# Eleven units of a second MLP product by seven block products instead of eight, on one Trainium2 core

## The chip, the cores and the metric

The kernel runs on one core of one Trainium2 chip. Five engines work beside each other: TensorE (PE, whose weight loads the profile lists as PEld), VectorE (DVE), ScalarE (ACT), GpSimd (POOL) and SyncE (SP, which issues the DMAs here). Each engine takes its instructions in an order that is fixed when the program is built, and waits on semaphores for the others. The metric is the device time of one execution in microseconds. The kernel before takes 416.2 us (median of three runs, 416.14 to 416.21).

## The reference

The input `x` has 2048 tokens of 448 columns. Its layer norm `xn` goes two ways, and everything is added up:

```python
x  = A_x
xn = _layernorm(x)
return x + A(xn) + B(xn)

def A(x):                       # a filter in the frequency domain
    X = rfft2(x); X = X * (w_r + 1j * w_i)
    return irfft2(X, s=(S, D))

def B(x):
    h  = gelu(layernorm(x) @ w1)
    # four column quarters shifted by +1, -1, +2, -2 tokens
    x1 = x + concat(shifted quarters of h) @ w2
    h2 = gelu(layernorm(x1) @ w3) @ w4      # w3: 448 x 1792, w4: 1792 x 448
    return x1 + h2
```

The change concerns only the last product, `gelu(...) @ w4`, for the last two groups of tokens.

## The kernel before

**Number format.** Every large product is made of three fp16 passes: each operand is split into a high and a low half, and high x high, high x low and low x high are added up in fp32 in PSUM (`PASS`). A split is one ACT copy to fp16 (the high half) and one DVE operation that subtracts it (the low half). `powers` forms powers of two that bring an operand into fp16's range; `s4` and `r4` are those of w4.

**The MLP.** The 2048 tokens are 16 blocks of 128, and a group `G` of 0 to 7 is two blocks. F = 1792 is cut into 14 chunks of 128, and a unit `(G, fp)` is one group with two chunks, so there are 8 x 7 = 56 units. A unit has two halves:

- `front(G, fp)` (L691) makes the hidden values: 22 matmuls of 256 columns (in `mlp_in`, L381) into a PSUM bank `pw` of tag "mm", of which there are two. Behind them ACT applies the gelu in place (L698) and copies the high half to `hf` (L700), and DVE makes the low half (L701).
- `back(G, fp)` (L705) multiplies by w4: for each of two blocks, two chunks and three passes, one matmul of 448 columns, 12 in all (L720), into two banks `acc` that add up over a group's seven units. In group 7 the last block is done in two column halves in two banks, so there are 6 matmuls of 448 columns and 12 of 224. Behind the group's last unit DVE adds the banks to the running sum `xt` (L726), and for groups 6 and 7 SP sends the block out (L729).

`mlp` (L731) issues the units of some groups in order, with `ahead` fronts in front of each back.

**The order of the work.** The program is written in stages, but each engine's order comes from a planner that simulates the program when it is built: of the instructions that are ready in its simulation, it takes the one of the lowest priority number. The stages' own instructions have the numbers of their place in the text; the MLP's matmuls have a high number (`FILL`), so that they fill what the stages leave free on PE; the copies behind a front have the lowest (`EVAC`). `behind(...)` makes an instruction wait in that order for another one.

**The stages around the change.** After the frequency filter's chunks comes the inverse transform: for each of the 16 blocks `inv_a` (L658, matmuls L663 into `pe`, banks of tag "tr", and sums in one of two buffers `stage0` and `stage1`, even blocks in the one and odd blocks in the other) and `inv_b` (L680, matmuls L684 into `py`, banks of tag "sp"), whose result is added to `xt`; `finish` (L494) sends blocks 0 to 11 out. The buffer `y1` (32 KB of each partition) is read for the last time in the inverse. In the text, `mlp(range(3, 6))` stands ahead of the inverse and `mlp(range(6, 8))` behind it, and then nothing follows. w4's split halves lie in `w4p`, and its raw values were loaded early in the kernel to `x2mem`, which later holds the transposed inputs of all fronts.

Of the kernel before, what the change touches and what calls it, by code (L numbers as in the profile page):

```python
# [12 lines left out]
F32 = mybir.dt.float32  # L13
F16 = mybir.dt.float16
I32 = mybir.dt.int32
AF = mybir.ActivationFunctionType
ALU = mybir.AluOpType
AX = mybir.AxisListType

S, D, DF, F = 2048, 448, 225, 1792  # L20
# [4 lines left out]
PASS = ((0, 0), (0, 1), (1, 0))  # L25
# [10 lines left out]
WMAX = [(1, 4), (1, 5), (1, 6), (2, 0), (2, 1), (2, 2), (2, 3), (2, 4)]  # L36
HS = 3
EVAC, FILL = 0, 100000

ME = [0, 224] + list(range(2, 224, 2))  # L40
MO = list(range(1, 224, 2))
# [78 lines left out]
def body(tc, nc, x, wf, w1, w2, w3, w4, c_g, c_n, c_small, out):  # L120
    V, A, P, T, SY = nc.vector, nc.scalar, nc.gpsimd, nc.tensor, nc.sync
    PSUM = bass.MemoryType.PSUM

    @contextlib.contextmanager
    def prio(base):
        kept = tc.cur_priority
        tc.cur_priority = max(base, at.get(base, 0))
        yield
        at[base] = tc.cur_priority
        tc.cur_priority = kept  # L130

    at = {}
    opened = {}

    def pool(name, bufs=1, side="left", space=None):
        kw = dict(name=name, bufs=bufs, reuse_waits="tile")
        if space is not None:
            kw["space"] = space
        else:
            kw["side"] = side  # L140
        cm = tc.tile_pool(**kw)
        opened[name] = cm
        return cm.__enter__()

    def close(name):
        opened.pop(name).__exit__(None, None, None)

    ps = pool("ps", space=PSUM)

    def bank(tag, name):  # L150
        return ps.tile([128, 512], F32, tag=tag, bufs=2, name=name)

    pc = pool("pc")
    px = pool("px")
    pw = pool("pw")
    pa = pool("pa")
# [3 lines left out]
    xt = [px.tile([128, 2, D], F32, name=f"xt{i}") for i in range(8)]  # L160

    def xb(b):
        return xt[b // 2][:, b % 2]
# [4 lines left out]
    def stage(name, n, side, dtype=F32):  # L168
        t = pw.tile([128, 1808], F32, tag=f"stage{side}", bufs=1, name=name)
        return (t if dtype is F32 else t.bitcast(dtype))[:, :n]  # L170
# [46 lines left out]
    x2mem = pw.tile([128, 9 * F], F16, name="x2mem")  # L217
    x2all = x2mem[:, 0:8 * F].rearrange("p (j t n) -> p j t n", j=4, t=7)
    w4raw = x2mem.bitcast(F32)[:, F:].rearrange("p (f n) -> p f n", f=14)
    w4v = w4.rearrange("(f p) n -> p f n", p=128)  # L220
# [16 lines left out]
        junk = xr.bitcast(F16) if junk is None else junk  # L237
        A.activation(out=junk[:src.shape[0], :n], in_=src, func=AF.Square, scale=2.0 ** -20, accum_out=col)

    def powers(m, n, key, tag="acc"):  # L240

        t = pc.tile([128, 2], F32, name=f"pt{key}")
        V.tensor_reduce(out=t[:, 0:1], in_=m[:, :n], axis=AX.X, op=ALU.add)
        pm = bank(tag, f"pm{key}") if isinstance(tag, str) else tag
        i = T.matmul(pm[:, 0:1], ones, t[:, 0:1], start=True, stop=True)
        after["p" + key] = (i.ins,)
        V.tensor_scalar(out=t[:, 1:2], in0=pm[:, 0:1], scalar1=2.0 ** -58, scalar2=None, op0=ALU.max)
        e = pc.tile([128, 3], I32, name=f"pe{key}")
        V.tensor_scalar(out=e[:, 0:1], in0=t.bitcast(I32)[:, 1:2], scalar1=1, scalar2=0x7F800000,
                        op0=ALU.logical_shift_right, op1=ALU.bitwise_and)  # L250
        V.tensor_scalar(out=e[:, 1:2], in0=e[:, 0:1], scalar1=-1, scalar2=185 << 23, op0=ALU.mult, op1=ALU.add)
        V.tensor_scalar(out=e[:, 2:3], in0=e[:, 0:1], scalar1=1, scalar2=69 << 23, op0=ALU.mult, op1=ALU.add)
        return e.bitcast(F32)[:, 1:2], e.bitcast(F32)[:, 2:3]

    def absmax(out_, in_):
# [2 lines left out]
    def split_w(hi, lo, src, s, low=None):  # L258
        if low is P:
            P.tensor_scalar(out=src, in0=src, scalar1=s, scalar2=0.0, op0=ALU.mult, op1=ALU.add)  # L260
            i = A.activation(out=hi, in_=src, func=AF.Copy)
            j = P.tensor_tensor(out=lo, in0=src, in1=hi, op=ALU.subtract)
            return i.ins, j.ins
        i = A.activation(out=hi, in_=src, func=AF.Copy, scale=s)
        j = V.scalar_tensor_tensor(out=lo, in0=src, scalar=s, in1=hi, op0=ALU.mult, op1=ALU.subtract)
        return i.ins, j.ins
# [86 lines left out]
    after = {}  # L353

    @contextlib.contextmanager
    def behind(*key):
        key = key if len(key) > 1 else key[0]
        with contextlib.ExitStack() as st:
            for i in after[key]:
                st.enter_context(tc.issue_after(i))  # L360
            yield
# [21 lines left out]


    w3p = pa.tile([128, 8, F], F16, name="w3p")
    w4p = {}

    w1p = p1.tile([128, 8, D], F16, name="w1p")
    w2p = pr.tile([112, 2, 4, D], F16, name="w2p")
# [299 lines left out]
    acc, hs = {}, {}  # L689

    def front(G, fp, tag):  # L691
        tok = slice(256 * (G % 2), 256 * (G % 2) + 256)
        pm = bank(tag, f"pw3_{G}{fp}")
        for ff in range(2):
            f = 2 * fp + ff
            mlp_in(pm[:, 256 * ff:256 * ff + 256], w3p, slice(128 * f, 128 * f + 128), x2all[:, G // 2], tok)
        with prio(EVAC):
            A.activation(out=pm, in_=pm, func=AF.Gelu_apprx_tanh, scale=r3)  # L698
            h = pw.tile([128, 2, 512], F16, tag="hf", bufs=3, name=f"hf{G}{fp}")
            i = A.activation(out=h[:, 0], in_=pm, func=AF.Copy, scale=h3)  # L700
            j = V.scalar_tensor_tensor(out=h[:, 1], in0=pm, scalar=h3, in1=h[:, 0], op0=ALU.mult, op1=ALU.subtract)  # L701
            after["f", G, fp] = i.ins, j.ins
        hs[G, fp] = h

    def back(G, fp):  # L705
        h = hs.pop((G, fp))
        if fp == 0:
            acc[G] = [bank("acc", f"acc{G}{i}") for i in range(2)]
            if G == 7:
                acc[G].append(bank("sp", "acc72"))  # L710
        for i in range(2):
            b = 2 * G + i
            c = D // 2 if b == NB - 1 else D
            parts = [(slice(o, o + c), acc[G][i + o // c][:, 0:c]) for o in range(0, D, c)]
            for r, to in parts:
                with behind("m", G, fp) if (G, fp) == (7, 6) and ("m", G, fp) in after else contextlib.nullcontext():
                    for f in (2 * fp, 2 * fp + 1):
                        for n, (hi, wi) in enumerate(((0, 0), (0, 1), (1, 0))):
                            o = 256 * (f % 2) + 128 * i
                            m = T.matmul(to, h[:, hi, o:o + 128], w4p[0][:, wi, f, r],  # L720
                                         start=f == 0 and n == 0, stop=f == 13 and n == 2)
                after["m", G, fp] = (m.ins,)
            if fp == 6:
                with prio(EVAC):
                    for r, to in parts:
                        V.scalar_tensor_tensor(out=xb(b)[:, r], in0=to, scalar=p34[:, min(G, 1):min(G, 1) + 1],  # L726
                                               in1=xb(b)[:, r], op0=ALU.mult, op1=ALU.add)
                        if G > 5:
                            SY.dma_start(ov[:, b, r], xb(b)[:, r])  # L729

    def mlp(Gs, hook=None, ahead=1, tags=("mm",)):  # L731
        with prio(FILL):
            todo = [(G, fp) for G in Gs for fp in range(7)]
            done = 0
            for n, (G, fp) in enumerate(todo):
                while done < min(n + 1 + ahead, len(todo)):
                    front(*todo[done], tags[done % len(tags)])
                    if hook:
                        with prio(EVAC):
                            hook(*todo[done])  # L740
                    done += 1
                back(G, fp)
# [9 lines left out]
    m1, m2, m3, m4 = (pc.tile([128, n], F32, name=f"m{i}") for i, n in ((1, 4), (2, 1), (3, 4), (4, 7)))  # L752
# [35 lines left out]
    with behind("n", 0):  # L788
        s1, r1 = powers(m1, 4, "1", "mm")
    h_alloc(0)  # L790
    first = [bank("mm" if k < 2 else "sp", f"pw1_0{k}") for k in range(4)]
# [51 lines left out]
    s3, r3 = powers(m3, 4, "3", "mm")  # L843
    h3 = pc.tile([128, 1], F32, name="h3")
# [22 lines left out]
        w1_unit(3, k)  # L867
    with behind("h", 3, 3):
        SY.dma_start(csm, c_small)
    s4, r4 = powers(m4, 7, "4")  # L870
    p34 = pc.tile([128, 2], F32, name="p34")
    V.scalar_tensor_tensor(out=p34[:, 1:2], in0=r3, scalar=2.0 ** 5, in1=r4, op0=ALU.mult, op1=ALU.mult)
    V.tensor_tensor(out=p34[:, 0:1], in0=p34[:, 1:2], in1=s12[:, 0:1], op=ALU.mult)
    w4p[0] = pa.tile([128, 2, 14, D], F16, tag="R", bufs=1, name="w4p")
    with behind(3, 1):
        w4_split(0)
    with behind(3, 3):
# [18 lines left out]
    pa2 = pool("pa2")  # L896
# [42 lines left out]
        if 0 <= i - 3 < NC:  # L939
            chunk_c(i - 3)  # L940
    close("pst")
    mlp(range(3, 6))
    pv = pool("pv", side="right")
    bs = [*range(8), *range(12, 16), *range(8, 12)]
    for n in range(17):
        if n in (0, 8):
            gather_u(n)
        if n < 16:
            inv_a(bs[n])
        if n:  # L950
            b = bs[n - 1]
            inv_b(b)
            if b < 12:
                finish(b)
    mlp(range(6, 8))
    for name in ("pv", "pa2", "pa", "pw", "px", "pc", "ps"):
        close(name)


# [22 lines left out]
```

## Time and profile before

| | |
|---|---|
| median of three runs | 416.2 us |
| the profiled execution | 416.43 us |
| its span, from the first instruction to the last | 414.6 us |
| granted TensorE clock, mean | 0.999 |
| instructions | 8472 |
| `front` matmuls (L381) | 1232, 151.7 us busy |
| `back` matmuls (L720) | 714, 139.7 us busy |
| inverse, from the first `pe` matmul to the last `py` | 284 to 338 us |
| MLP alone on PE | 339 to 411 us |
| from the last `back` matmuls' start (36 of them) | 406.8 us |

How to read it: the page gives the busy time of each engine, 40 equal slices of the span, the chain of work that ended last (followed back from the last instruction), and groups of instructions with count, busy time, mean duration and the idle time ahead of them. Matmul durations are modelled and overlap, so the distance between the starts of steps says more than the busy time. In the chain and the timeline a row is a run of like instructions: start, length, engine, what it writes, line, count.

### The profile page before, as it was taken

How to read it: one execution, taken by the hardware profiler on the slowest of the kernel's cores; microseconds unless marked ns; L12 is line 12 of the kernel's file. 1: busy time of each engine (PE TensorE's matmuls, PEld its weight loads, DVE VectorE, ACT ScalarE, POOL GpSimd, SP SyncE). 2: the span in 40 equal slices, each digit the busy share in tenths (PEclk: the TensorE clock that was granted, in tenths of full speed). 3: DMA queues.
4: the chain of work that ended last, by engine and by line, in shares of the span. 5: the costliest groups of instructions: out<-in, count | busy, mean ns of one | idle time of the engine just before them, and what ended most of it. 6: DMA issues, size and time to landing. Idle time of an engine off the chain costs nothing.

```text
span 414.6 us, 8472 instructions
## 1 busy us (share of the span) xinstructions
PE 407.9 (98%) x3313; PEld 290.4 (70%) x3313; DVE 294.3 (71%) x613; ACT 246.1 (59%) x428; POOL 97.2 (23%) x172
## 2 busy tenths in 40 slices
PE   8999999999989999999999999999999999999996
PEld 3655555765658777776888887877777766777885
DVE  4888899798866879854799888857999934112122
ACT  4698879973758876643689888854344533222321
POOL 3876710102245947400021122110000000000000
PEclk9999999999999999999999999999999999999999
DMA  8959879914867557315256655500111011001001
GB/s 275 350 189 177 159 148 323 158 59 90 186 166 206 153 183 221 90 47 141 70 149 163 168 144 141 127 27 2 69 46 66 2 47 44 2 0 46 2 0 46
DMA packets 54536, 48.53 MB, mean 117 GB/s; under 512 B 37536, under 2 KB 48864, under 8 KB 54496
## 3 DMA queue, kind: packets, MB, share of 16 engines
q1 hardware_dynamic: 54496, 47.99, 43.6%
q8 instruction: 26, 0.43, 0.4%
q14 instruction: 14, 0.11, 0.1%
HBM read 35.52 MB, written 3.67 MB: 95 GB/s over the span
## 4 chain that ended last, share of the span: by engine, by line
PE 68%; DVE 12%; ACT 7%; issue 4%; DMA 4%; POOL 2%; SPq 1%; DVEq 0%; POOLq 0%; ACTq 0%
PE pw L381 26%; PE acc L720 25%; PE pw L410 4%; PE ps L539 3%; PE pe L663 2%; PE wps L749 2%; PE py L684 2%; ACT te L619 2%; DVE xt L452 2%; DMA x2mem<-y 2%; DMA x2mem<-w 1%; PE pu L642 1%; PE pp L597 1%; DVE y L484 1%; PE px L614 1%
## 5 line engine op out<-in xcount | busy, mean ns | idle before, releaser
L381 PE MATMUL pw<-x2mem,w3p 128*128 128x256 f16 x1232 | 151.7, 273 | 0.0
L720 PE MATMUL acc<-w4p,hf 128*128 128x448 f16 (+1 forms) x714 | 139.7, 341 | 1.4 <-DVE hf L701 1.4
L381 PEld LDWEIGHTS <-w3p 128*128 128x128 f16 x1232 | 119.0, 98 | 22.4
L720 PEld LDWEIGHTS <-hf 128*128 128x128 f16 x714 | 69.2, 98 | 49.9 <-DVE hf L701 1.8
L701 DVE SCALAR_TENSOR_TENSOR hf<-pw,h,hf 128x512 f16<-128x512 f32 x56 | 41.8, 747 | 64.1 <-ACT hf L700 63.7
L698 ACT ACTIVATE pw<-pw,pe 128x512 f32<-128x512 f32 x56 | 36.7, 656 | 76.8 <-PE pw L381 76.6
L450 PE MATMUL pw<-w2p,h 112*128 112x448 f16 x192 | 39.9, 352 | 0.7 <-DMA h<-hs 0.7
L700 ACT ACTIVATE hf<-pw,h 128x512 f16<-128x512 f32 x56 | 38.3, 687 | 1.5
L410 PE MATMUL pw<-w1p,xT 128*128 128x448 f16 x176 | 35.4, 352 | 0.0
L623 POOL TENSOR_TENSOR z<-te 128x450 f32<-128x450 f32 x16 | 15.7, 982 | 69.5 <-DVE te L621 69.5
L450 PEld LDWEIGHTS <-h 112*128 112x128 f16 x192 | 18.6, 98 | 17.2 <-DMA h<-hs 1.0
L410 PEld LDWEIGHTS <-xT 128*128 128x128 f16 x176 | 16.9, 98 | 16.4 <-DVE xT L375 0.8
L604 ACT ACTIVATE pf<-pp 64x450 f16<-64x450 f32 x32 | 17.4, 543 | 12.6 <-DVE pf L605 8.3
L605 DVE TENSOR_TENSOR pf<-pp,pf 64x450 f16<-64x450 f32 x32 | 19.9, 622 | 4.3 <-ACT pf L604 3.9
L522 POOL TENSOR_TENSOR f<-xr 128x452 f32<-128x452 f32 x16 | 18.4, 1173 | 0.6
L619 ACT ACTIVATE te<-px 64x450 f32<-64x450 f32 x32 | 17.3, 540 | 1.1 <-PE px L614 0.6
L726 DVE SCALAR_TENSOR_TENSOR xt<-acc,p,xt 128x448 f32<-128x448 f32 (+1 forms) x17 | 10.9, 651 | 8.6 <-PE acc L720 8.3
L530 DVE TENSOR_TENSOR xh<-f,xh 128x452 f16<-128x452 f32 x16 | 12.6, 828 | 5.5 <-ACT xh L529 5.5
L519 POOL TENSOR_TENSOR xr<-xf 128x452 f32<-128x452 f32 x8 | 9.9, 1236 | 26.0 <-issue 20.2
L529 ACT ACTIVATE xh<-f 128x452 f16<-128x452 f32 x16 | 8.4, 571 | 10.3 <-POOL f L522 10.2
L684 PE MATMUL py<-vh,csm 128*128 128x448 f16 x48 | 14.0, 352 | 0.0
L663 PE MATMUL pe<-csm,U 113*128 113x113 f16 (+1 forms) x192 | 13.7, 213 | 0.0
(164 smaller groups left out, 572.5 us busy)
## 6 DMA issues: line engine op xcount, KB each, us to landing
wc<-wf SPq DMA_DIRECT2D x32, 225.0 KB, 3.7
wl<-wf SPq DMA_DIRECT2D x8, 450.0 KB, 4.0
xt<-x SPq DMA_DIRECT2D x8, 448.0 KB, 9.0
xf<-x SPq DMA_DIRECT2D x8, 448.0 KB, 3.9
loads<-x SPq DMA_DIRECT2D x7, 448.0 KB, 3.7
out<-xt SPq DMA_DIRECT2D x13, 224.0 KB, 1.9
w3raw<-w SPq DMA_DIRECT2D x3, 896.0 KB, 13.7
gn<-c_g SPq DMA_DIRECT2D x16, 128.0 KB, 3.1
```

The costliest lines, as they stand in the source:

```text
L381: T.matmul(ps_out, wp[:, wi + t, cols], xT[:, xi + t, tok], start=t == 0 and wi + xi == 0, stop=t == 3 and wi == 4)
L410: T.matmul(pm[:, :D], xTs[g][:, xi + t, 128 * i:128 * i + 128], w1p[:, wi + t], start=t == 0 and p == 0, stop=t == 3 and p == 2)
L450: T.matmul(pm[:, :D], hT[g][:112, 4 * hi + k, o:o + 128], w2p[:, wi, k], start=n == 0, stop=n == 11)
L522: P.tensor_tensor(out=f[:, :, k:k + 2].rearrange("p b s d -> p s b d"), in0=u[:, :, 0], in1=u[:, :, 1], op=op)
L605: V.tensor_tensor(out=lo, in0=src, in1=hi, op=ALU.subtract)
L619: A.activation(out=e[64 * h:64 * h + 64], in_=px_[64 - 64 * h:128 - 64 * h, :2 * DF], func=AF.Copy)
L663: T.matmul(pe[:, 113 * q:113 * q + 113], U[b // 8 * 8][ui][:kd, q, b % 8, :], cI[ii][:kd, 113 * q:113 * q + 113], start=n == 0, stop=n == 2)
L684: T.matmul(py[:, :D], cV[ri], vh[:, vi], start=n == 0, stop=n == 2)
L698: A.activation(out=pm, in_=pm, func=AF.Gelu_apprx_tanh, scale=r3)
L700: i = A.activation(out=h[:, 0], in_=pm, func=AF.Copy, scale=h3)
L701: j = V.scalar_tensor_tensor(out=h[:, 1], in0=pm, scalar=h3, in1=h[:, 0], op0=ALU.mult, op1=ALU.subtract)
L720: m = T.matmul(to, h[:, hi, o:o + 128], w4p[0][:, wi, f, r], start=f == 0 and n == 0, stop=f == 13 and n == 2)
```

## The change

Six units of group 6 (all but the last) and five of group 7 (0, 1, 2, 4, 5) multiply by w4 in another way. A unit is a product of a 2 x 2 block matrix (two token blocks by two chunks, blocks of 128 x 128) with another (two chunks by two column halves, blocks of 128 x 224). The plain way takes eight block products; the new one takes seven, of sums and differences of blocks, and adds their results up.

- `sums` takes the place of the copies behind such a unit's front: the gelu goes from PSUM to an fp32 buffer `g` in SBUF, two DVE operations form the sums, and the high and low halves (`hz`) are made of all seven operands, 896 columns instead of 512.
- `w4_sums` loads a pair of w4's chunks again (448 KB) into `stage0` or `stage1`, forms their differences and sums with four DVE operations of 224 columns, and splits the 896 columns. This is done for six pairs of chunks, behind the units (5,4), (5,5), (5,6), (6,0), (6,1) and (6,3). The results lie in parts of `x2mem` and of w4's buffer that are free by then. w4's scale is one power of two smaller, to leave room for the sums.
- `seven` takes the place of `back` for these units: 7 x 3 = 21 matmuls of 224 columns. Four of the products add up over the units in two more banks (`side`, of tag "tr" in group 6 and "sp" in group 7), and behind a group's last such unit five DVE operations add them to `xt`. Group 7's third bank moves from "sp" to "tr".
- Group 5 is issued behind the inverse, and its two blocks go out behind its last unit instead of in `finish`. `y1` is given up ahead of it, and its place is taken by the new buffers `g` and `hz`.
- Groups 6 and 7 are issued with two fronts ahead of each back instead of one, and with one for unit (7,5). Group 7's order is 0, 1, 2, 4, 5, 3, 6, so that its last two units are plain ones.

```diff
+SEVEN = {6: [0, 1, 2, 3, 4, 5], 7: [0, 1, 2, 4, 5]}
+ORD = {G: list(range(7)) for G in range(6)} | {6: list(range(7)), 7: [0, 1, 2, 4, 5, 3, 6]}
...
+    def sums(G, fp, pm):
+        g = pz.tile([128, 12, 128], F32, tag="g", bufs=2, name=f"g{G}{fp}")
+        q = g.rearrange("p (a r) n -> p a r n", r=3)
+        A.activation(out=q[:, 0:2, 0:3:2].rearrange("p t f n -> p f t n"),
+                     in_=pm.rearrange("p (f t n) -> p f t n", f=2, t=2), func=AF.Gelu_apprx_tanh, scale=r3)
+        V.tensor_tensor(out=q[:, 2:4, 0], in0=q[:, 0:2, 0], in1=q[:, 0:2, 2], op=ALU.add)
+        V.tensor_tensor(out=q[:, 0:3, 1], in0=q[:, 1:4, 0], in1=q[:, 0:3, 0], op=ALU.subtract)
+        h = pz.tile([128, 2, 7 * 128], F16, tag="hz", bufs=3, name=f"hz{G}{fp}")
+        src = g[:, 1:8].rearrange("p a n -> p (a n)")
+        i = A.activation(out=h[:, 0], in_=src, func=AF.Copy, scale=h3)
+        j = V.scalar_tensor_tensor(out=h[:, 1], in0=src, scalar=h3, in1=h[:, 0], op0=ALU.mult, op1=ALU.subtract)
...
+    def w4_sums(j, part):
+        t = part.rearrange("p (k n) -> p k n", n=DH)
+        SY.dma_start(t.rearrange("p (f k) n -> p f (k n)", f=2), w4v[:, 2 * j:2 * j + 2])
+        def go():
+            for o, i, k, op in ((3, 3, 1, ALU.subtract), (1, 1, 0, ALU.subtract),
+                                (0, 3, 0, ALU.add), (2, 2, 0, ALU.subtract)):
+                V.tensor_tensor(out=t[:, o], in0=t[:, i], in1=t[:, k], op=op)
+            split_w(w4t[j][:, 0], w4t[j][:, 1], t, s4)
+        return go
...
+    def seven(G, fp):
...
+        for blk, to, b, new in ((2, m1, w(0, 0), lead), (4, a1[:, 0:DH], w(1, 0), begins), (1, a2[:, 0:DH], t4, begins),
+                                (6, a12, w(1, 1), begins and G == 7), (5, m5, t1, lead), (3, m6, t2, False),
+                                (0, m7, t3, False)):
+            for n, (hi, wi) in enumerate(PASS):
+                m = T.matmul(to, h[:, hi, 128 * blk:128 * blk + 128], b[wi], start=new and n == 0,
+                             stop=last and n == 2 and blk in (2, 5, 3, 0), skip_group_check=True)
+        if last:
+            x = xt[G].rearrange("p b (k n) -> p (b k) n", k=2)
+            wide = lambda m, n: m.unsqueeze(1).to_broadcast([128, n, DH])
+            for to, m in ((x, wide(m1, 4)), (x[:, 0:2], wide(m6, 2)), (x[:, 3], m6), (x[:, 1:4:2], wide(m5, 2)),
+                          (x[:, 0:2], wide(m7, 2))):
+                V.scalar_tensor_tensor(out=to, in0=m, scalar=p34[:, 1:2], in1=to, op0=ALU.mult, op1=ALU.add)
...
-    mlp(range(3, 6))
+    mlp(range(3, 5))
...
-            if b < 12:
+            if b < 10:
                 finish(b)
-    mlp(range(6, 8))
+    close("pa2")
+    pz = pool("pz")
+    LATE = [(0, 5, 4), (1, 5, 5), (2, 5, 6), (3, 6, 0), (4, 6, 1), (5, 6, 3)]
...
+    mlp([5], hook=w4_late)
+    mlp(range(6, 8), hook=w4_late, ahead=2)
```

More of the change, by code (lines that the diff above doesn't have):

```diff
@@ L38 @@
 EVAC, FILL = 0, 100000
+DH = D // 2
+SEVEN = {6: [0, 1, 2, 3, 4, 5], 7: [0, 1, 2, 4, 5]}
+ORD = {G: list(range(7)) for G in range(6)} | {6: list(range(7)), 7: [0, 1, 2, 4, 5, 3, 6]}
 ME = [0, 224] + list(range(2, 224, 2))
@@ L238, in squares, with powers @@
         A.activation(out=junk[:src.shape[0], :n], in_=src, func=AF.Square, scale=2.0 ** -20, accum_out=col)
-    def powers(m, n, key, tag="acc"):
+    def powers(m, n, key, tag="acc", spare=0):
         t = pc.tile([128, 2], F32, name=f"pt{key}")
@@ L250, in powers @@
                         op0=ALU.logical_shift_right, op1=ALU.bitwise_and)
-        V.tensor_scalar(out=e[:, 1:2], in0=e[:, 0:1], scalar1=-1, scalar2=185 << 23, op0=ALU.mult, op1=ALU.add)
-        V.tensor_scalar(out=e[:, 2:3], in0=e[:, 0:1], scalar1=1, scalar2=69 << 23, op0=ALU.mult, op1=ALU.add)
+        V.tensor_scalar(out=e[:, 1:2], in0=e[:, 0:1], scalar1=-1, scalar2=185 - spare << 23, op0=ALU.mult, op1=ALU.add)
+        V.tensor_scalar(out=e[:, 2:3], in0=e[:, 0:1], scalar1=1, scalar2=69 + spare << 23, op0=ALU.mult, op1=ALU.add)
         return e.bitcast(F32)[:, 1:2], e.bitcast(F32)[:, 2:3]
@@ L385, in body @@
     w3p = pa.tile([128, 8, F], F16, name="w3p")
-    w4p = {}
+    w4p, w4t = {}, {}
     w1p = p1.tile([128, 8, D], F16, name="w1p")
@@ L697, in front @@
         with prio(EVAC):
+            if fp in SEVEN.get(G, ()):
+                hs[G, fp] = sums(G, fp, pm)
+                return
             A.activation(out=pm, in_=pm, func=AF.Gelu_apprx_tanh, scale=r3)
@@ L703, in front @@
         hs[G, fp] = h
+    def sums(G, fp, pm):
[9 more added lines that the diff above has]
+        j = V.scalar_tensor_tensor(out=h[:, 1], in0=src, scalar=h3, in1=h[:, 0], op0=ALU.mult, op1=ALU.subtract)
+        after["f", G, fp] = i.ins, j.ins
+        return h
@@ new lines, in body @@
+    side = {}
+    def seven(G, fp):
+        h = hs.pop((G, fp))
+        lead, last = fp == SEVEN[G][0], fp == SEVEN[G][-1]
+        if lead:
+            side[G] = [bank("sp" if G == 7 else "tr", f"side{G}{i}") for i in range(2)]
+        m1, m6, m5, m7 = (side[G][i][:, DH * k:DH * k + DH] for i in range(2) for k in range(2))
+        a2, a1 = acc[G][0], acc[G][1]
+        a12 = acc[G][2][:, 0:DH] if G == 7 else a1[:, DH:D]
+        w = lambda f, k: [w4p[0][:, i, 2 * fp + f, DH * k:DH * k + DH] for i in range(2)]
+        t2, t1, t4, t3 = ([w4t[fp][:, i, k] for i in range(2)] for k in range(4))
+        begins = fp == ORD[G][0]
+        for blk, to, b, new in ((2, m1, w(0, 0), lead), (4, a1[:, 0:DH], w(1, 0), begins), (1, a2[:, 0:DH], t4, begins),
[4 more added lines that the diff above has]
+                             stop=last and n == 2 and blk in (2, 5, 3, 0), skip_group_check=True)
+        after["m", G, fp] = (m.ins,)
+        if last:
[4 more added lines that the diff above has]
+                V.scalar_tensor_tensor(out=to, in0=m, scalar=p34[:, 1:2], in1=to, op0=ALU.mult, op1=ALU.add)
@@ L705, in back @@
     def back(G, fp):
-        h = hs.pop((G, fp))
-        if fp == 0:
+        first, end = fp == ORD[G][0], fp == ORD[G][-1]
+        if first:
             acc[G] = [bank("acc", f"acc{G}{i}") for i in range(2)]
             if G == 7:
-                acc[G].append(bank("sp", "acc72"))
+                acc[G].append(bank("tr", "acc72"))
+        if fp in SEVEN.get(G, ()):
+            seven(G, fp)
+            return
+        h = hs.pop((G, fp))
         for i in range(2):
@@ L715, in back @@
             for r, to in parts:
-                with behind("m", G, fp) if (G, fp) == (7, 6) and ("m", G, fp) in after else contextlib.nullcontext():
+                with behind("m", G, fp) if G == 7 and end and ("m", G, fp) in after else contextlib.nullcontext():
                     for f in (2 * fp, 2 * fp + 1):
-                        for n, (hi, wi) in enumerate(((0, 0), (0, 1), (1, 0))):
+                        for n, (hi, wi) in enumerate(PASS):
                             o = 256 * (f % 2) + 128 * i
                             m = T.matmul(to, h[:, hi, o:o + 128], w4p[0][:, wi, f, r],
-                                         start=f == 0 and n == 0, stop=f == 13 and n == 2)
+                                         start=first and f % 2 == 0 and n == 0, stop=end and f % 2 == 1 and n == 2,
+                                         skip_group_check=G in SEVEN)
                 after["m", G, fp] = (m.ins,)
-            if fp == 6:
+            if end:
                 with prio(EVAC):
@@ L727, in back @@
                                                in1=xb(b)[:, r], op0=ALU.mult, op1=ALU.add)
-                        if G > 5:
+                        if G > 4:
                             SY.dma_start(ov[:, b, r], xb(b)[:, r])
@@ L732, in mlp @@
         with prio(FILL):
-            todo = [(G, fp) for G in Gs for fp in range(7)]
+            todo = [(G, fp) for G in Gs for fp in ORD[G]]
             done = 0
             for n, (G, fp) in enumerate(todo):
-                while done < min(n + 1 + ahead, len(todo)):
+                while done < min(n + 1 + (ahead if todo[n] != (7, 5) else 1), len(todo)):
                     front(*todo[done], tags[done % len(tags)])
@@ L869, in body @@
         SY.dma_start(csm, c_small)
-    s4, r4 = powers(m4, 7, "4")
+    s4, r4 = powers(m4, 7, "4", spare=1)
     p34 = pc.tile([128, 2], F32, name="p34")
@@ L873, in body @@
     V.tensor_tensor(out=p34[:, 0:1], in0=p34[:, 1:2], in1=s12[:, 0:1], op=ALU.mult)
-    w4p[0] = pa.tile([128, 2, 14, D], F16, tag="R", bufs=1, name="w4p")
+    w4mem = pa.tile([128, 8 * F], F16, tag="R", bufs=1, name="w4p")
+    w4p[0] = w4mem[:, 0:28 * D].rearrange("p (i f n) -> p i f n", i=2, f=14)
+    homes = {4: x2mem[:, 8 * F:9 * F], 5: w4mem[:, 28 * D:28 * D + F]}
+    for j in range(4):
+        homes[j] = x2mem[:, F * j:F * j + F]
+    w4t.update({j: m.rearrange("p (i k n) -> p i k n", i=2, k=4) for j, m in homes.items()})
     with behind(3, 1):
@@ L952, in body, with w4_late @@
             inv_b(b)
-            if b < 12:
+            if b < 10:
                 finish(b)
-    mlp(range(6, 8))
-    for name in ("pv", "pa2", "pa", "pw", "px", "pc", "ps"):
+    close("pa2")
+    pz = pool("pz")
+    LATE = [(0, 5, 4), (1, 5, 5), (2, 5, 6), (3, 6, 0), (4, 6, 1), (5, 6, 3)]
+    def w4_late(G, fp):
+        for n, (j, *at) in enumerate(LATE):
+            if at == [G, fp]:
+                go = w4_sums(j, stage(f"late{j}", 896, n % 2))
+                with behind("f", G, fp):
+                    go()
+    mlp([5], hook=w4_late)
+    mlp(range(6, 8), hook=w4_late, ahead=2)
+    for name in ("pv", "pz", "pa", "pw", "px", "pc", "ps"):
         close(name)
```

## The prediction

> **What bounds the kernel now.** First the busy shares on the page and their course over the span, then the stretches by stage, then the chain that ended last.
>
> ```profile
> PE 407.9 (98%) x3313; PEld 290.4 (70%) x3313; DVE 294.3 (71%) x613; ACT 246.1 (59%) x428; POOL 97.2 (23%) x172
> ...
> PEclk9999999999999999999999999999999999999999
> ```
>
> ```profile
> 283.00:339.00 56.00, 56.00 (x511) 40.80 (x510) 48.84 (x117) 24.03 (x48) 0.00 (x0) 1.00 0.11 42
> 339.00:411.00 72.00, 72.00 (x562) 54.57 (x561) 15.70 (x23) 20.25 (x30) 0.00 (x0) 1.00 0.04 14
> ```
>
> The columns of the second fence are length, then busy time of PE, PEld, DVE, ACT and POOL, the granted clock, the DMA share and GB/s. From 339 us on, PE is never idle at full clock; DVE works 15.7 of 72 us and ACT 20.25. A busy PE is modelled, so the chain must say whether its steps really abut:
>
> ```profile
> 350.70 2.27 PE acc L720 x12
> ...
> 369.39 2.27 PE acc L720 x12
> 371.66 2.40 PE pw L381 x22
> 374.06 2.27 PE acc L720 x12
> 376.33 2.40 PE pw L381 x22
> ...
> 388.09 2.29 PE acc L720 x18
> 390.38 2.40 PE pw L381 x22
> ...
> 406.84 4.58 PE acc L720 x36
> ```
>
> They do: each start plus its length is the next start, and the chain holds nothing but `front` (L381, 2.40 us) and `back` (L720, 2.27 us in group 6, about 2.286 us in group 7). Time taken out of `back` there shortens the span one for one, as long as nothing else comes late. In the inverse before it (283 to 339 us) PE is full too, so putting group 5's code behind the inverse can't fill a gap; I cost that move at nothing, since either order has the same matmuls to fill with.
>
> **The products.** A plain unit is 12 matmuls of 448 columns: 2.27/12 = 0.189 us each. Seven products in three passes are 21 matmuls of 224 columns. Group 7 already runs that shape: of the 18 matmuls, 6 are 448 wide and 12 are 224 wide, each with its own weight load. 2.286 - 6 x 0.189 = 1.151 us for 12, or 0.0959 us each. So a unit by seven products takes 21 x 0.0959 = 2.014 us.
>
> - Group 6, six units: 6 x (2.27 - 2.014) = 1.54 us less.
> - Group 7, five units: 5 x (2.286 - 2.014) = 1.36 us less.
>
> Together 2.90 us, all on PE's path.
>
> A finer matmul needs more weight loads, and that is where a rule speaks against the change:
>
> ```profile
> L720 PEld LDWEIGHTS <-hf 128*128 128x128 f16 x714 | 69.2, 98 | 49.9 <-DVE hf L701 1.8
> ...
> 273.38 1.34 PE pu L642 x24
> ```
>
> If a load of 98 ns could not overlap its neighbour, 21 of them would set 2.058 us per unit, and the gain would be 6 x 0.212 + 5 x 0.228 = 2.41 us. But 24 matmuls of 128 columns, each with a load, start within 1.34 us, 56 ns apart, so loads of 98 ns do overlap; I take 0.0959. The Trainium skill ("TensorE: Matmul & The Clock Gate", LDWEIGHTS) gives columns / 1.2 ns, 107 ns for 128 columns; by it a unit would take 2.24 us and the gain would be 0.4 us. The trace's 56 ns spacing disagrees with that as a pace.
>
> **The units' own sums, off PE.** The plain chain behind a `front` (which ends at 359.88, where the next `back` starts), and the nearest rows for the new operations:
>
> ```profile
> 359.88 2.43 PE L720 MATMUL acc<-w4p,hf 128*128 128x448 f16 x12
> 362.15 2.56 PE L381 MATMUL pw<-x2mem,w3p 128*128 128x256 f16 x22
> 364.56 2.43 PE L720 MATMUL acc<-w4p,hf 128*128 128x448 f16 x12
> ```
>
> ```profile
> 360.09 0.66 ACT L698 ACTIVATE pw<-pw,pe 128x512 f32<-128x512 f32 x1 [3.29 <-PE pw L381]
> 360.78 0.69 ACT L700 ACTIVATE hf<-pw,h 128x512 f16<-128x512 f32 x1
> 361.50 0.75 DVE L701 SCALAR_TENSOR_TENSOR hf<-pw,h,hf 128x512 f16<-128x512 f32 x1 [3.92 <-ACT hf L700]
> ```
>
> ```profile
> L265 DVE SCALAR_TENSOR_TENSOR w4p<-x2mem,pe,w4p 128x896 f16<-128x896 f32 x7 | 7.9, 1134 | 0.0
> ...
> L726 DVE SCALAR_TENSOR_TENSOR xt<-acc,p,xt 128x448 f32<-128x448 f32 x15 | 10.1, 678 | 8.5 <-PE acc L720 8.3
> ...
> L673 DVE TENSOR_TENSOR e<-e 128x226 f32<-128x226 f32 x16 | 6.0, 388 | 0.1
> ...
> L773 DVE TENSOR_TENSOR x<-xt,x 128x384 f16<-128x384 f32 x4 | 2.2, 548 | 0.0
> ...
> L726 DVE SCALAR_TENSOR_TENSOR xt<-acc,p,xt 128x224 f32<-128x224 f32 x2 | 0.9, 446 | 0.1
> ```
>
> ```profile
> L264 ACT ACTIVATE w4p<-x2mem,pe 128x896 f16<-128x896 f32 x7 | 6.8, 1031 | 2.7 <-DVE pe L251 2.7
> ```
>
> Per unit: gelu 0.66 (ACT), an add of 256 columns, between 0.388 and 0.548, 0.42 by its width (DVE), a subtract of 384 columns 0.55 (DVE), the 896-wide copy 1.03 (ACT), the 896-wide rest 1.13 (DVE). With 0.2 us from the front's end to the gelu and some 0.05 us per hand-over the chain is 0.2 + 0.66 + 0.42 + 0.55 + 1.03 + 1.13 + 0.2 = 4.2 us, against 2.4 us now (from 359.88 to 362.25). What hides it: `ahead=2` puts a unit's `back` two fronts and two backs behind its own front, 2 x 2.40 + 2 x 2.01 = 8.8 us. Cover left: 4.6 us. With one front ahead the cover would be 4.4 us and 0.2 us would be left. Cost on the path: 0. PSUM is no bound there: `pw` has two banks and a bank is free after the gelu, since the sums stand in SBUF.
>
> DVE gets 2.10 us per unit in place of 0.75, ACT 1.69 in place of 1.35, out of a unit's 4.41 us on PE.
>
> **w4's sums.** Six times: a DMA of 448 KB, four operations of 224 columns on DVE (4 x 0.388 = 1.55), the split (1.03 on ACT, 1.13 on DVE): 2.68 us of DVE each. When could they start?
>
> ```profile
> 333.35 1.15 DVE L677 SCALAR_TENSOR_TENSOR vh<-e,vh 128x448 f16<-128x448 f32 x2
> ```
>
> ```profile
> loads<-x SPq DMA_DIRECT2D x7, 448.0 KB, 3.7
> ...
> x2mem<-w SPq DMA_DIRECT2D x2, 672.0 KB, 10.0
> ```
>
> The two `stage` buffers are free when the inverse's last `vh` are made, 334.5 us. A load of that size lands in 3.7 us: pairs 0 and 1 are there at 338.2. One buffer then turns over in 3.7 + 1.55 + 1.03 + 1.13 = 7.4 us, two buffers give one pair per 3.7 us, and PE wants one per 4.41 us. By the chain's rows the first `back` of group 6 stands at 350.7; with a third front ahead of it that becomes about 353, and pair 0 is ready at 338.2 + 3.7 = 342. Ten us to spare; cost 0. On SP's queue these six loads stand ahead of the outputs of blocks 10 and 11, for which nobody waits until the end. The two outputs and final sums of those blocks move from the inverse to behind group 5; they run beside group 6's fronts, cost 0.
>
> On DVE a sum that waits for its load holds up the unit copies queued behind it. Those have 4.6 us of cover in groups 6 and 7 and 2.2 us in group 5 (362.25 against the `back` at 364.56), and the loads of pairs 0 and 1 land ahead of or near their turn, so I cost this at 0; without the cover it is one load, up to 3.7 us, once.
>
> **The five final adds per group.** One of 896 columns (1.13), three of 448 (0.68), one of 224 (0.45): 3.6 us of DVE. In group 7 they start behind unit 5 and have front (7,6), 2.40, and two plain backs, 4.57 us, ahead of the end: hidden, and the tail stays as it is. In group 6 they stand ahead of its two final sums (2 x 0.68), and these free the banks for group 7. Between the end of `back` (6,5) and the start of `back` (7,0) lie two fronts and a plain back, 7.07 us. DVE must do there 3.6 + 1.36, the rest of unit (7,0)'s copy (1.13) and the sums of unit (7,1) (0.97): 7.06 us. Just full. Its end could come 1.13 us late if (7,1)'s copy goes first, and nothing late if a further front is put in between; back-to-back operations start about 0.08 us sooner than the durations add up to, so I take 0.2 us.
>
> **DVE in the whole stretch of group 6.** Six units 12.6, four of w4's pairs 10.7, the five adds 3.6, final sums 1.36, the copies of (6,6) 0.75 and (7,0) 2.10: 31.1 us, against about 6 x 4.41 + 4.67 = 31.1 us on PE. By durations that is full; less 0.08 for each of some 49 operations it is 27, or 87%. The pairs come early and units 4 and 5 carry none, so a backlog is worked off before the adds. That is the weakest place of the change.
>
> The scale's spare bit is other constants in the same operations: 0. Eleven units' third bank of group 7 in another tag: 0.
>
> **Sum.** The profiled execution took 416.43 us, 0.23 above the median of 416.2. 416.43 - 1.54 - 1.36 + 0.2 = 413.7; against the median 413.5.
>
> **The rivals.**
> 1. DVE gets in the way in part: the hand-over from group 6 to group 7 costs its 1.13 us, and the three units that carry a pair of w4's, (6,0), (6,1) and (6,3), 2.10 + 2.68 = 4.78 us of DVE against 4.41, cost up to 0.37 each. 416.2 - 2.9 + 1.1 to 2.2: 414.4 to 415.5. For it: the full count above. Against it: 4.6 us of cover and the earlier starts.
> 2. Weight loads set the pace of the 224-wide matmuls: 416.2 - 2.41 = 413.8, or with the 0.2 us 414.0. Against it: the 56 ns spacing. The Trainium skill's rule on LDWEIGHTS, above, is the same mechanism at 107 ns.
> 3. The gain comes to nothing, since PE's order was fixed for other times and what `back` frees returns as PE waiting for hz: 2.90 us of waits, 0.26 per unit. 415.4 to 417.0. Against it: each hz has 4.6 us.
> 4. The other side: w4's loads land late. At 10 us a load, as the 672 KB row, one buffer turns over in 13.7 us. Pair 0 and 1 ready at 348.3, 2 and 3 at 362, 4 and 5 at 376; units 4 and 5 want theirs at about 353 + 4 x 4.41 = 370.6 and 375. Unit 4 would wait 5 us: 416.2 - 2.9 + 5 = 418. It decides where a load takes over about 8 us. For it: the loads run one buffer at a time. Against it: the 10 us row is from a stretch full of loads, and here the DMA share is 0.04. DVE would stand at the head of its queue meanwhile, with hz behind it. The Trainium skill ("Perfetto Trace Analysis", Tensor Engine Instruction) says that DVE and ACT are strict FIFO; no row here contradicts it.
>
> **How the numbers follow.** Forecast, 413.2 to 413.9: 0.60. Rival 1: 0.17. Rival 2: 0.05. Rival 3: 0.06. Rival 4, or its like on DVE: 0.12. About 0.2% (0.8 us) is what a measurement of this kernel can tell from no change: faster means below 415.4, slower above 417.0. Faster: 0.60 + 0.17 + 0.05 = 0.82; same 0.06; slower 0.12. The range reaches from the full gain with no stall and 0.3 us of scatter, 412.9, past rival 1 to the near edge of rival 3, 415.7, and leaves out 0.17 above. The forecast's own range is 413.2 to 413.9.
>
> **What would show it.** Backs of group 6 as 21 matmuls in 2.01 us each, starts abutting with fronts of 2.40; a unit's period 4.41 us; DVE about 27 us busy in group 6's 31; w4's loads near 3.7 us; no PE or weight load waiting for DVE or ACT over 0.3 us; the tail from the last matmul to the end unchanged. Wrong it would be by a `back` over 2.1 us, by PE waiting on hz or on w4's sums, by the wait ahead of `back` (7,0), or by time lost ahead of 339 us, where another order of the inverse would have to show as PE idle.

## The result, and the profile after

The changed kernel takes 413.1 us (median of four runs, 412.93 to 413.58) against 416.2: a ratio of 0.9934, 95% interval 0.9921 to 0.9947. Measured again, against the kernel before on the same chip (415.8 us there), it took 412.9 us, ratio 0.9928 (0.9915 to 0.9941). The two intervals together span 2.2 to 3.5 us less. The forecast was 413.5, with 413.2 to 413.9 as its own range.

The profile after, in the same views. First the stretch from 338.24 us to the last matmul's end, then the parts of the chain that ended last:

```profile
338.24:407.79 69.55, 69.54 (x633) 61.17 (x631) 49.91 (x80) 29.37 (x37) 0.00 (x0) 1.00 0.14 41
```

```profile
361.21 0.29 PE side L756 x3
361.50 0.86 PE acc L756 x9
362.36 0.86 PE side L756 x9
363.22 2.40 PE pw L384 x22
...
376.46 2.40 PE pw L384 x22
378.87 2.27 PE acc L785 x12
381.13 2.40 PE pw L384 x22
383.54 0.29 PE side L756 x3
...
403.21 4.58 PE acc L785 x36
407.79 0.02 issue
```

PE is still never idle, and each step begins where the one ahead of it ends. A back by seven products takes 0.29 + 0.86 + 0.86 = 2.01 us where a plain one takes 2.27 (378.87, unit (6,6)), and a unit's period is 4.41 us (361.21 + 2.01 + 2.40 = 365.62). DVE's busy time in this stretch is three times what it was (49.9 of 69.6 us), and none of that ends a wait of PE.

How much of the two profiles' difference is the change? The profiled executions took 416.43 and 412.93 us, 3.50 us apart. Both wait once at 119 us, in a part where PE's order is the same in both. In the timeline of PE, before and then after:

```profile
120.87 1.69 PE L720 MATMUL acc<-w4p,hf 128*128 128x448 f16 x8 [1.35 <-DVE hf L701]
...
123.48 0.28 PE L539 MATMUL ps<-csm,xh 128*128 128x128 f16 x2
```

```profile
120.18 1.69 PE L785 MATMUL acc<-w4p,hf 128*128 128x448 f16 x8 [0.61 <-DVE hf L707]
...
122.79 0.28 PE L542 MATMUL ps<-csm,xh 128*128 128x128 f16 x2
```

That wait differs by 0.74 us between these two executions, and of the change only w4's scale and the size of its buffer lie ahead of it. From the first `ps` matmul to the end of the last `back` it is 411.42 - 123.48 = 287.94 us before and 407.79 - 122.79 = 285.00 us after: 2.94 us less. The full sum of the products was 2.90.

### The profile page after: what moved, and what is told of

Same layout as the page of the kernel before. It is cut to its first block, busy times and chain, and to the rows that moved or that the text cites. A ratio compares the mean times of both kernels' runs of the same rounds, so it can differ in the third digit from the quotient of the medians.

```text
span 411.1 us, 8687 instructions
## 1 busy us (share of the span) xinstructions
PE 404.9 (98%) x3382; PEld 296.8 (72%) x3382; DVE 329.5 (80%) x675; ACT 256.0 (62%) x434; POOL 96.8 (24%) x172
## 4 chain that ended last, share of the span: by engine, by line
PE 65%; DVE 13%; ACT 8%; issue 6%; DMA 5%; POOL 2%; SPq 1%; POOLq 0%; DVEq 0%; ACTq 0%
PE pw L384 26%; PE acc L785 19%; PE side L756 3%; PE ps L542 3%; PE pw L413 2%; PE pe L666 2%; PE acc L756 2%; PE py L687 2%; ACT te L622 2%; DVE xt L455 1%; PE pu L645 1%; DMA x2mem<-w 1%; PE pp L600 1%; DVE y L487 1%; PE px L617 1%
## 5 line engine op out<-in xcount | busy, mean ns | idle before, releaser
L785 PE MATMUL acc<-w4p,hf 128*128 128x448 f16 (+1 forms) x552 | 112.7, 348 | 0.6 <-DVE hf L707 0.6
L785 PEld LDWEIGHTS <-hf 128*128 128x128 f16 x552 | 53.5, 98 | 40.5 <-DVE hf L707 1.0
L704 ACT ACTIVATE pw<-pw,pe 128x512 f32<-128x512 f32 x45 | 29.4, 654 | 35.6 <-PE pw L384 35.4
L707 DVE SCALAR_TENSOR_TENSOR hf<-pw,h,hf 128x512 f16<-128x512 f32 x45 | 33.5, 746 | 15.2 <-ACT hf L706 14.9
L706 ACT ACTIVATE hf<-pw,h 128x512 f16<-128x512 f32 x45 | 30.7, 685 | 1.1
L756 PEld LDWEIGHTS <-hz 128*128 128x128 f16 x231 | 22.2, 98 | 0.2
L722 ACT ACTIVATE hz<-g,h 128x896 f16<-128x896 f32 x11 | 11.5, 1041 | 14.3 <-DVE g L719 14.3
L723 DVE SCALAR_TENSOR_TENSOR hz<-g,h,hz 128x896 f16<-128x896 f32 x11 | 12.6, 1150 | 5.1 <-ACT hz L722 4.9
```

The lines of the kernel that those rows point to most:

```text
L756: m = T.matmul(to, h[:, hi, 128 * blk:128 * blk + 128], b[wi], start=new and n == 0, stop=last and n == 2 and blk in (2, 5, 3, 0), skip_gr ...
L785: m = T.matmul(to, h[:, hi, o:o + 128], w4p[0][:, wi, f, r], start=first and f % 2 == 0 and n == 0, stop=end and f % 2 == 1 and n == 2, sk ...
```

## The experiments

**The parts alone.** Where does the gain sit: in the products of group 7, in those of group 6, or in the order that came with them?

```diff
-SEVEN = {6: [0, 1, 2, 3, 4, 5], 7: [0, 1, 2, 4, 5]}
+SEVEN = {7: [0, 1, 2, 4, 5]}                 # group 7 alone
+SEVEN = {6: [0, 1, 2, 3, 4, 5]}              # group 6 alone
+SEVEN = {}                                   # none, and LATE = [] (no sums of w4)
```

> Only the five units of group 7 go by seven products; group 6 stays plain, w4's sums are still formed. If the whole gain is PE time of the products, 1.36 us of it is group 7's: about 414.8 us, 1.4 us below the kernel before, and each of those backs 2.01 us. If the order of the stages or the second front ahead brought the gain, this kernel has both and should come near 413.1.

> Only the six units of group 6 go by seven products; group 7 stays plain in its new order. If the gain is PE time of the products: 1.54 us less than before, about 414.6 us. If DVE were a hidden limit in the crowded group 6, the gain here would be clearly below 1.5 us while group 7 alone gave its full 1.36 us.

> No unit by seven products and no sums of w4; group 5 behind the inverse, two fronts ahead in groups 6 and 7, and group 7's new order stay. If these moves cost and bring nothing, as the prediction has it: 416.2 us, as before, within 0.2 us. If the part of the gain above 2.9 us (413.1 measured, 413.3 by the full sum) came from the moves, 415.8 us or less.

| | median us | ratio to before (415.6) | interval | less than before, us |
|---|---|---|---|---|
| group 7 alone | 414.5 | 0.9973 | 0.9963 to 0.9982 | 1.1 (1.36 forecast) |
| group 6 alone | 414.2 | 0.9965 | 0.9953 to 0.9977 | 1.5 (1.54 forecast) |
| neither, order kept | 415.5 | 0.9995 | 0.9987 to 1.0004 | 0.1, not told from 0 |

Both parts bring what their matmuls save, within the intervals, and together 2.6 us. The new order of group 5, the second front ahead and group 7's new order bring and cost nothing that can be measured.

**Weight loads.** The kernel before, with the backs of group 6 cut into halves:

```diff
             parts = [(slice(o, o + c), acc[G][i + o // c][:, 0:c]) for o in range(0, D, c)]
+            if G == 6:
+                parts = [(slice(o, o + D // 2), acc[G][i][:, o:o + D // 2]) for o in (0, D // 2)]
...
```

> The kernel before, with the plain backs of group 6 cut into 24 matmuls of 224 columns in place of 12 of 448; no other change. It doubles the weight loads and keeps the columns. At 0.0959 us per 224-wide matmul a back takes 2.30 us instead of 2.27: 7 x 0.03 = 0.2 us more, 416.4 us. If weight loads of 98 ns set the pace, 2.35 us and 0.6 us more, 416.8 us; at 107 ns 2.57 us and 2.1 us more, 418.3 us.

415.6 us against 415.5, ratio 1.0000 (0.9991 to 1.0009). Its chain:

```profile
354.92 2.30 PE acc L722 x24
357.22 2.40 PE pw L381 x22
359.62 2.30 PE acc L722 x24
```

24 matmuls with 24 loads take 2.30 us, as 0.0959 us each gives, and not 2.35 or 2.57. Twice the loads cost 0.03 us a back, too little to measure in the whole.

**One front ahead.**

```diff
-    mlp(range(6, 8), hook=w4_late, ahead=2)
+    mlp(range(6, 8), hook=w4_late, ahead=1)
```

> As the changed kernel, but with one front ahead of each back in groups 6 and 7. By the prediction's sum the cover falls from 8.8 to 4.4 us against a chain of 4.2 us: nothing is lost in group 7, where DVE is free, and in group 6, where w4's sums stand on DVE too, up to 1.5 us is lost as PE waiting for hz: 413.1 to 414.6 us. If the second front ahead is not what hides the chain, 413.1 us and no such wait.

413.4 us, ratio 0.9949 (0.9931 to 0.9967), against 0.9928 and 0.9934 with two. The intervals overlap, and from 347 us on the table of waits of its profiled execution shows none of PE's matmuls. The chain of that execution shows how:

```profile
361.47 3.06 PE pw L384 x28
364.53 0.19 PE side L756 x2
364.72 0.38 PE acc L756 x4
365.10 0.19 PE side L756 x2
365.30 0.33 PE pw L384 x3
365.62 0.10 PE side L756
```

The planner starts a back with the two passes that need only the high half, and puts matmuls of the next front in between until the low half is there. So a unit's chain is also hidden by the order within units. The expected loss of up to 1.5 us in group 6 was not there. The profiled execution is the shortest of six, though (412.66 us); another took 415.28 us with a mean granted clock of 0.996, and what held that one up is not known, so a loss in some executions is not ruled out.

**DVE's room.** The low halves of hz are made twice and three times, with the same result:

```diff
         j = V.scalar_tensor_tensor(out=h[:, 1], in0=src, scalar=h3, in1=h[:, 0], op0=ALU.mult, op1=ALU.subtract)
+        j = V.scalar_tensor_tensor(out=h[:, 1], in0=src, scalar=h3, in1=h[:, 0], op0=ALU.mult, op1=ALU.subtract)
```

> As the changed kernel, but the low halves of hz are made twice: 1.07 us more of DVE in each of the eleven units. By the prediction's count DVE's work in group 6 is 27 us by starts against 31 us of PE; with 6 to 7 times 1.07 us more it is 34 us, over by 3, and part of that must show: 414 to 416 us, as PE waiting for hz or for the banks in group 6, while group 7 (3.1 us of DVE per unit against 4.41) loses nothing. If DVE has much more room than counted, 413.1 us.

> As the changed kernel, but the low halves of hz are made three times: 2.1 us more of DVE in each of the eleven units. In the profile after, DVE is busy 24.7 of the 31 us from 350 to 381 and 13.4 of the 23 us from 381 to 404; made twice it was 29.0 of 31 and lost nothing. A third time needs some 34 of 31 us in group 6 and 24 of 23 in group 7: if DVE's work is what would bound there, 2 to 5 us are lost, 415 to 418 us, as PE waiting for hz or for the banks. If something else hides DVE's work, 413.1 us again.

Twice: 413.1 us, ratio 0.9943 (0.9931 to 0.9955), no loss that can be told from the change itself. Three times: 420.2 us, ratio 1.0106 (1.0093 to 1.0119), 7.3 us more than the change. The same 31 us of group 6 in the change, with the halves made twice, and three times (columns as before):

```profile
350.00:381.00 31.00, 31.00 (x293) 28.17 (x292) 24.71 (x42) 15.91 (x19) 0.00 (x0) 1.00 0.12 37
```

```profile
350.00:381.00 31.00, 31.00 (x295) 28.37 (x294) 29.00 (x45) 15.94 (x19) 0.00 (x0) 1.00 0.14 38
```

```profile
350.00:381.00 31.00, 25.98 (x236) 23.24 (x234) 30.82 (x45) 13.80 (x17) 0.00 (x0) 0.94 0.11 35
```

DVE can be 94% busy here and PE doesn't notice; when it is full, PE stands. The loss is larger than the 2 to 5 us expected, and the timeline and the stretches of this run show one reason:

```profile
368.09 0.37 PE L758 MATMUL side<-w4p,hz 128*128 128x224 f16 x1 [3.52 <-DVE hz L725]
...
370.49 0.58 PE L758 MATMUL side<-w4p,hz 128*128 128x224 f16 x2
...
371.56 1.36 PE L384 MATMUL pw<-x2mem,w3p 128*128 128x256 f16 x11
```

```profile
368.00:372.00 4.00, 3.91 (x25) 3.32 (x26) 4.00 (x9) 2.02 (x3) 0.00 (x0) 0.61 0.00 0
372.00:376.00 4.00, 4.00 (x42) 3.79 (x40) 4.00 (x6) 2.96 (x4) 0.00 (x0) 1.00 0.01 4
```

Behind a wait of 3.52 us the granted clock is 0.61 for 4 us: the unit's 21 matmuls take 371.56 - 368.09 = 3.47 us instead of 2.01. So this wait costs 3.5 + 1.5 us, and two others 0.64 and 0.86. The rest of the 7.3 us I did not place piece by piece.

**Late loads of w4.** Each pair is loaded twice or three times, one load behind the other:

```diff
         SY.dma_start(t.rearrange("p (f k) n -> p f (k n)", f=2), w4v[:, 2 * j:2 * j + 2])
+        SY.dma_start(t.rearrange("p (f k) n -> p f (k n)", f=2), w4v[:, 2 * j:2 * j + 2])
```

> As the changed kernel, but each pair of w4's chunks is loaded twice, one load behind the other, so a pair is there about 7 us after its buffer is free. By the prediction's turnover the last pairs are ready at 368 us against a need at 370 and 375 us (2.9 us earlier in this kernel's own time is the same on both sides): no loss, 413.1 us. If the loads were near the limit already, PE waits for w4's sums at units 2 to 5 of group 6, 414 us or more.

> As before this one with three loads for one, about 10.5 us from a free buffer to the last landing. The prediction has the point from which loads decide at about 8 us, and 5 us lost at 10 us: 416 to 420 us, with PE waiting for the sums of w4 at group 6's units 2 to 5. If the planner can put other work in front of the wait, less: there are at most three finished fronts to take, so above 414 us still.

Twice: 417.4 us, ratio 1.0049 (1.0035 to 1.0062), where no loss was expected. Three times: 426.2 us, ratio 1.0256 (1.0239 to 1.0273), more than expected too. DVE, and then PE, in the run with two loads:

```profile
345.82 0.75 DVE L707 SCALAR_TENSOR_TENSOR hf<-pw,h,hf 128x512 f16<-128x512 f32 x1
352.48 0.39 DVE L736 TENSOR_TENSOR late<-late 128x224 f32<-128x224 f32 x1 [5.90 <-DMA late<-w]
352.79 0.42 DVE L718 TENSOR_TENSOR g<-g 128x256 f32<-128x256 f32 x1
```

```profile
345.85 0.93 PE L786 MATMUL acc<-w4p,hf 128*128 128x448 f16 x4 [1.75 <-ACT hf L706]
355.76 0.36 PE L757 MATMUL side<-w4p,hz 128*128 128x224 f16 x2 [2.34 <-ACT hz L722]
357.01 0.37 PE L757 MATMUL side<-w4p,hz 128*128 128x224 f16 x1 [0.31 <-DVE hz L723]
```

DVE stands for 5.90 us at the first sum of pair 2, whose load isn't there. Behind it in the queue are unit (6,0)'s own sums (L718), which need nothing of that pair, and PE waits 2.34 + 0.31 us for the copies made of them. The 1.75 us lie ahead of that stand and come from the loads of pairs 0 and 1, by way of ACT: it stands for 5.82 us at the high halves of their sums (L267), with the gelu (L704) and the copy (L706) of a unit of group 5 behind them:

```profile
342.33 2.20 ACT L267 ACTIVATE x2mem<-late,pe 128x896 f16<-128x896 f32 x2 [5.82 <-DVE late L736]
344.43 0.64 ACT L704 ACTIVATE pw<-pw,pe 128x512 f32<-128x512 f32 x1
345.11 0.69 ACT L706 ACTIVATE hf<-pw,h 128x512 f16<-128x512 f32 x1
```

Together PE waits 4.40 us in this execution, all of it for copies of hidden values, and loses about 1.5 us more at a lower clock behind the last wait (last section). This execution is the longest of the four, 418.47 us; the median's loss against 413.1 is 4.3 us. Nothing waits for w4 in units 2 to 5. With three loads both kinds of wait appear: in that profile PE waits 3.45 us for hf, 1.51 and 3.59 us for hz, and behind the last of these 0.63 us for a pair's high half, so at that place the two causes can't be told apart. To tell the place in the queue from late products, the same two loads with the sums of pairs 2 to 5 gated later:

```diff
-    LATE = [(0, 5, 4), (1, 5, 5), (2, 5, 6), (3, 6, 0), (4, 6, 1), (5, 6, 3)]
+    LATE = [(0, 5, 4), (1, 5, 5), (2, 6, 1), (3, 6, 2), (4, 6, 3), (5, 6, 4)]
```

> As the run with each pair of w4's chunks loaded twice (417.4 us), but the sums of pairs 2 to 5 are gated one to three units later, behind (6,1), (6,2), (6,3) and (6,4), so that unit (6,0)'s own sums stand ahead of them in DVE's queue. If the 4.3 us were lost because DVE stood at the head of its queue waiting for pair 2's load, with the first units' sums and group 5's final sums behind it, most of it comes back: 413 to 414.5 us, with no wait of PE for hz at the start of group 6. If it was lost because the products of units 2 to 5 got their w4 too late, nothing comes back: 417 us or more.

413.9 us, ratio 0.9961 (0.9948 to 0.9973): 3.5 of the 4.3 us come back. In its table of waits the longest one of DVE for these loads is 2.3 us, and from 330 us on PE has no wait for hz:

```profile
DVE late L736 <- DMA late<-w: 4.8, 3, 2.3
```

PE doesn't wait for hf either, but that the edit can't claim: it leaves pairs 0 and 1 as they were, and their loads were all there 7.9 us after their buffers came free in this run (at 341.05 us) against 9.5 us in the other (341.60). What the edit shows is the wait at the start of group 6: with two loads that came from the place of pair 2's sums in DVE's queue, and not from the time at which w4's sums are ready.

## Why the prediction was right, and where it was not

- **The products.** 0.0959 us per matmul of 224 columns, read off group 7's plain backs, gave 2.014 us per back; it is 2.01. The sum of 2.90 us is 2.94 in the two profiles and lies within the 2.2 to 3.5 us of the runs; each group alone brings its part.
- **The weight loads.** Rival 2 is out: 24 loads in 2.30 us. The Trainium skill's 107 ns ("TensorE: Matmul & The Clock Gate", LDWEIGHTS) would have made that 2.57 us; as a load's own duration it is near the 98 ns of the rows, but it is not the pace.
- **The move of group 5 and the new order cost nothing.** Right (0.9995), and it brings nothing.
- **The hand-over from group 6 to group 7.** I took 0.2 us off. There is no such wait: back (7,0) starts at 383.54, where the front ahead of it ends. DVE's work ahead of it ends in time:

```profile
376.21 1.87 DVE L764 SCALAR_TENSOR_TENSOR xt<-side,p,xt 128x896 f32<-128x896 f32 x2
...
381.60 1.27 DVE L792 SCALAR_TENSOR_TENSOR xt<-acc,p,xt 128x448 f32<-128x448 f32 x2
```

  The final sums end at 382.87, 0.67 us ahead. I had let the five adds start at the end of back (6,5); the first two start already at 376.21, while that back's last matmuls are still running (its step in the chain ends at 376.46). This term is 0.2 of the 0.4 us between 413.5 and the 413.1 measured, which lies 0.1 us below the forecast's own range; the other 0.2 is less than the interval can tell.
- **Two fronts ahead as the cover.** The chain is as summed (4.2 us): a front of group 7 that ends at 387.79 has its hz complete at 392.04, 4.25 us later. Rival 3 is out, since PE has no wait in the profile after from 338 us on. That it needs the second front is not shown: with one, nothing measurable was lost.
- **DVE in group 6.** I had 27 us by starts in 31. Pair 2 was done ahead of that stretch (its split ends at 348.60), and the row says 24.7. Rival 1's mechanism is real, as the run with three times the halves shows, but its point lies 4 us of DVE work or more away from the change.
- **Late loads, rival 4.** The forecast stood because the loads take 3.5 us, near the 3.7 of the rows of the same size; DVE still stands 2.20 us for pair 0's load in the changed kernel, at 335.09, and no wait of PE follows. The point of decision, about 8 us, was wrong: with two loads pair 2 is there 7.8 us after its buffer came free (3.54 and 4.25 us for the two), where I had counted no loss, and the change is already slower than the kernel before. I priced the delay of units 2 to 5, with a turnover of the buffers, and put the place in DVE's queue at 0 because of 4.6 us of cover, and at one load at most without it. What failed is that step: the waiting sum has the next units' copies behind it, the first backs of group 6 want these before anything of pair 2, and 2.65 us of a stand of 5.90 us reached PE. ACT's queue, where the pairs' high halves hold up copies in the same way, I had not priced at all. The Trainium skill's strict FIFO of DVE ("Perfetto Trace Analysis", Tensor Engine Instruction), which I named beside that rival, is what the rows show: L718 waits behind L736.

## What to carry to other kernels

Where one engine is never idle in a stage and its steps abut in the chain, taking columns off its matmuls pays one for one, and the price of the new shape is best read from a place where the kernel already runs it. What pays for it on another engine can be free as long as that engine has room: here DVE's work cost nothing at 94% of the stretch and 7.3 us when it was full. Count it against the stage, and not against the span. Put work that waits for a transfer behind the copies that the bound engine needs next: an in-order engine passes a late transfer on to everything queued behind it.

## What the runs showed of the hardware that I had not expected

PE's clock answers to one wait of a few microseconds. In the run with three times the low halves it is 0.61 of full speed over the 4 us behind a wait of 3.52 us, and full again behind that, so the wait cost 5.0 us. In the run with two loads less was enough: behind the waits of 2.34 and 0.31 us, with 0.94 us of PE's work between them, it is halved for 3 us and full again from 361 us on (columns as before):

```profile
345.00:350.00 5.00, 4.15 (x30) 2.86 (x31) 1.46 (x2) 1.45 (x3) 0.00 (x0) 1.00 0.71 207
357.00:360.00 3.00, 2.99 (x16) 2.40 (x17) 3.00 (x8) 1.27 (x3) 0.00 (x0) 0.50 0.02 5
361.00:364.00 3.00, 3.00 (x32) 2.80 (x30) 3.00 (x4) 2.11 (x3) 0.00 (x0) 1.00 0.45 125
```

Half of 3 us, 1.5 us, is my estimate of what this execution lost beside its waits. The wait of 1.75 us, which ends at 345.85, left the clock at 1.00. The Trainium skill ("TensorE: Matmul & The Clock Gate", Part 1) has half the clock after an idle window of about 3.4 us, and full speed again after a busy one. The halved clock and the wait of 3.52 us agree with it; the run with two loads shows that no unbroken wait of that length is needed. So two waits of 2.65 us together cost more than themselves here.
